# Turning the exponentials of pooled attention in five pieces of 127 and 68 keys instead of six of 96

## The chip, the cores and the metric

One core of a Trainium2 chip runs the whole program. The metric is the device time of one execution in microseconds, as the median of the runs shown; a profile of one further execution gives the rows.

## The reference

Three layers follow each other. Attention comes first, with keys and values pooled by 8, so that each of 8 batches has 8 heads, 576 queries and only 72 keys:

```python
Sp = S // pool                                   # 576 // 8 = 72
k_p = k.reshape(B, H, Sp, pool, D).mean(axis=3)
v_p = v.reshape(B, H, Sp, pool, D).mean(axis=3)
scores = scale * np.matmul(q, k_p.transpose(0, 1, 3, 2))
scores = scores - np.max(scores, axis=-1, keepdims=True)
attn = np.exp(scores)
attn = attn / (np.sum(attn, axis=-1, keepdims=True) + 1e-09)
return np.matmul(attn, v_p).astype(np.float32)
```

Its output, 4608 tokens of 512 numbers, goes through a layer of 8 experts that takes the best one for each token, and then through a second one that takes the best two. Both expert layers multiply by `w1`, take a relu, and multiply by `w2`.

## The kernel before, in words

The attention stage goes over the 4608 tokens in 36 tiles of 128 tokens (a batch is 4.5 tiles, so every ninth tile has its tokens from two batches). The rest of the run is the two expert layers. The order of instructions on every engine is the order in which the code is written; nothing is moved by a scheduler, and waits are put in where a tile's buffer is read or used again.

One step of the attention loop, for token tile t, puts these on TensorE (PE), in this order:

- `transp(t)`: the exponentials of tile t, 128 tokens by 8 heads x 72 keys, are 576 columns. They are turned in six pieces of 96 columns, three into PSUM bank 3 and three into bank 4. ScalarE (ACT) copies each bank to SBUF (`et`, 96 x 384). A piece of 96 keys spans parts of two heads.
- `scores(t+3, 0)`: four heads' scores of a later tile, 4 passes.
- `av(t)`: for each half of the heads (`hb`, 4 heads), three matmuls of the turned exponentials with the prepared `v` block `vb`, into bank 5 or 6. An f32 matmul of this kind is two passes in the trace, a turn is one.
- `scores(t+3, 1)`: the other four heads.
- jobs of the batch to come. In three successive steps ahead of a batch's first tile they are: `place_v` (ACT copies the pooled `v` into a padded layout, two copies), then `prep_v` for half 0, then `prep_v` for half 1. One `prep_v` is four matmuls into bank 7, and one ACT copy that moves the result into `vb`.

ACT does, in one step, the two copies of `transp(t)`, the eight exponentials of tile t+2 (`expo`), and issues the store of tile t-1. VectorE (DVE) takes the maxima, and divides by the sums.

A call of `bank(k)` is a new use of PSUM bank k: its first writer waits until all readers of the bank's last use are through. That is what `bank(3 + hb)` in `transp` and `bank(7)` in `prep_v` do.

Of the kernel before, what the change touches and what calls it, by code (L numbers as in the profile page):

```python
# [41 lines left out]
def kernel(ctx: ExitStack, tc: tile.TileContext, a: dict):  # L42
# [61 lines left out]
    von = rp.tile([96, 6, 2], F32, name="von")  # L104
# [576 lines left out]
    with actx:  # L681
# [7 lines left out]
        for n, t in enumerate((kb[0], vp[0], rc, *kb[1:], *vp[1:])):
            (V if n < 3 else G).memset(t, 0.0)  # L690
        for h in range(2):
            r = slice(64 * h, 64 * h + 64)
            w0 = (1 + h) * VW
            A.activation(rc[r, :, w0:w0 + D], ident[r, 64 * h:64 * h + D].unsqueeze(1).to_broadcast([D, 4, D]), AF.Copy)
            A.activation(rc[r, :, w0 + D:w0 + D + E], wg1[r], AF.Copy)
        for t in vb:
            G.memset(t[96:97], 0.0)
            for c in (0, 2, 3, 5):
                G.memset(t[96:97, c, VW - 1, :], 1e-9)
            G.tensor_copy(t[0:96, :, VW - 1, :], von)  # L700
        for t in (*etb[0], *etb[1]):
            G.memset(t[96:97], 1.0)
# [284 lines left out]
        for t in range(NT):  # L987
# [265 lines left out]
def host_arrays(inp):  # L1253
# [27 lines left out]
    vo = np.zeros((6 * 96, 2), f)  # L1281
    for c in range(6):
        for s in range(96):
            h = (96 * c + s) // 72
            vo[96 * c + s, h - (c % 3) - 4 * (c // 3)] = 1
    r["vones"] = vo.reshape(6, 96, 2).transpose(1, 0, 2)
# [31 lines left out]
```

## Time and profile before

| | |
|---|---|
| median of 3 runs | 1511.95 us (1509.63 to 1512.92) |
| the profiled execution: its own time | 1503.11 us |
| the profiled execution: span from first to last instruction | 1501.4 us |
| PE busy over the span | 1450.4 us, 97% |
| ACT, DVE, POOL busy over the span | 80%, 78%, 60% |
| attention stage: first to last turn of exponentials | 19.5 us to 163.8 us |

The profiled execution is 8.8 us below the median of the runs, of which 1.7 us are outside its span. Busy shares of PE count a matmul until its result is out, and matmuls follow each other before that; so what one costs in a stream is the distance from its start to the next one's start, and not its duration.

### The profile page before, as it was taken

What the parts mean: (1) busy time and instruction counts of PE and PEld (TensorE: products, weight loads), DVE (VectorE), ACT (ScalarE), POOL (GpSimd) and SP (SyncE); (2) the same over time, 40 slices, a digit from 0 to 9 for tenths busy, and PEclk for the clock granted to TensorE, in tenths of its full rate; (3) what the DMA queues carried; (4) which work ended last, traced back from release to release, by engine and by line L of the source; (5) the groups of instructions that cost most, each with busy time, mean ns of one, the idle gap of its engine ahead of it and who ended that gap; (6) DMA issues with size and microseconds to landing.
All of it is one profiled execution on the core that took longest, in us unless ns stands there. A gap on an engine that the chain in (4) does not pass through costs nothing.

```text
span 1501.4 us, 31172 instructions
## 1 busy us (share of the span) xinstructions
PE 1450.4 (97%) x7485; PEld 1206.7 (80%) x7485; DVE 1177.1 (78%) x2990; ACT 1194.4 (80%) x3155; POOL 901.3 (60%) x1065
## 2 busy tenths in 40 slices
PE   5999889999999999999999999999999999999996
PEld 5998768888888888778888888788888888888885
DVE  4778747777777777778888888888888888888883
ACT  5777558888888888778888888888888888888882
POOL 7677757888878888555454444544545444454442
PEclk9999999999999999999999999999999999999999
DMA  8866665655666565544434444344443444434432
GB/s 303 307 236 246 191 186 149 162 159 159 163 155 160 159 163 149 138 107 100 93 87 104 92 105 94 85 106 92 95 102 87 106 92 100 97 87 105 92 99 31
DMA packets 146685, 200.55 MB, mean 134 GB/s; under 512 B 71953, under 2 KB 104977, under 8 KB 143825
## 3 DMA queue, kind: packets, MB, share of 16 engines
q1 hardware_dynamic: 112032, 139.11, 30.6%
q0 software_dynamic: 24688, 49.94, 17.2%
q10 hardware_dynamic: 9792, 9.44, 1.9%
q8 instruction: 80, 1.31, 0.4%
q14 instruction: 93, 0.75, 0.2%
HBM read 121.64 MB, written 62.26 MB: 122 GB/s over the span
## 4 chain that ended last, share of the span: by engine, by line
issue 45%; POOL 29%; POOLq 6%; DMA 5%; PE 5%; DVE 5%; ACT 5%; SPq 0%; ACTq 0%; DVEq 0%
POOL out L453 8%; POOL w2l L223 6%; POOL l_d L187 4%; POOLq L174 3%; ACT xt L289 2%; POOL w1l L223 2%; POOL x L250 2%; POOL nz L254 2%; DMA x_d<-xr 1%; POOLq L223 1%; DMA x3t<-x 1%; POOL cur L244 1%; DVE g2t L393 1%; PE bank L294 1%; POOL x L358 1%
## 5 line engine op out<-in xcount | busy, mean ns | idle before, releaser
L312 DVE STREAM_TRANSPOSE ht<-h 32x256 f32<-32x256 f32 x1136 | 495.3, 436 | 96.6 <-ACT h L305 81.9
L289 ACT ACTIVATE xt<-xz 32x128 f32<-32x128 f32 x1728 | 531.2, 307 | 41.4 <-DVE xz L282 20.2
L294 PE MATMUL bank<-w1h,xh 128*128 (+1 forms) x904 | 357.9, 396 | 3.5 <-ACT xh L274 3.5
L295 PE MATMUL bank<-w1l,xh 128*128 (+1 forms) x904 | 355.2, 393 | 0.0
L296 PE MATMUL bank<-w1h,xl 128*128 (+1 forms) x904 | 354.3, 392 | 0.6 <-DVE xl L278 0.6
L296 PE MATMUL bank<-w2h,hl 128*128 (+1 forms) x896 | 351.7, 393 | 2.2 <-DVE hl L321 1.1
L295 PE MATMUL bank<-w2l,hh 128*128 (+1 forms) x896 | 351.5, 392 | 0.0
L294 PE MATMUL bank<-w2h,hh 128*128 (+1 forms) x896 | 350.7, 391 | 0.0
L223 POOL TENSOR_TENSOR w1l<-sg,w1h 128x512 f32 x109 | 140.7, 1291 | 239.4 <-ACT w1h L220 236.6
L453 POOL DMA_INDIRECT out<-yo,cur x76 | 121.0, 1592 | 161.5 <-ACT yo L450 157.3
L294 PEld LDWEIGHTS bank<-w1h,xh 128*128 128x128 f32 x904 | 170.1, 188 | 40.5 <-ACT xh L274 4.1
L296 PEld LDWEIGHTS bank<-w2h,hl 128*128 128x128 f32 x896 | 168.3, 188 | 42.4 <-DVE hl L321 4.3
L296 PEld LDWEIGHTS bank<-w1h,xl 128*128 128x128 f32 x904 | 170.0, 188 | 38.6 <-DVE xl L278 1.7
L295 PEld LDWEIGHTS bank<-w1l,xh 128*128 128x128 f32 x904 | 170.3, 188 | 35.3
L294 PEld LDWEIGHTS bank<-w2h,hh 128*128 128x128 f32 x896 | 168.3, 188 | 37.4
L295 PEld LDWEIGHTS bank<-w2l,hh 128*128 128x128 f32 x896 | 168.3, 188 | 36.4
L305 ACT ACTIVATE h<-bank 128x512 f32<-128x512 f32 x226 | 132.2, 585 | 55.3 <-PE bank L296 51.5
L223 POOL TENSOR_TENSOR w2l<-sg,w2h 128x512 f32 x109 | 141.5, 1298 | 14.6 <-ACT w2h L220 13.6
L250 POOL DMA_INDIRECT x<-x_d,cur x113 | 124.1, 1098 | 36.1 <-POOL cur L244 33.2
L278 DVE TENSOR_TENSOR xl<-xt,xh 128x512 fp32r<-128x512 f32 x108 | 75.8, 702 | 72.7 <-ACT xh L274 58.6
L320 ACT ACTIVATE hh<-ht 128x1024 fp32r<-128x1024 f32 x71 | 75.5, 1063 | 58.3 <-DVE ht L312 58.3
L187 POOL DMA_INDIRECT l_d<-le,dst x74 | 77.8, 1052 | 52.0 <-DVE dst L443 38.8
(267 smaller groups left out, 1970.2 us busy)
## 6 DMA issues: line engine op xcount, KB each, us to landing
sg<-w SPq DMA_DIRECT2D x118, 512.0 KB, 3.7
x_d<-zt SPq DMA_DIRECT2D x46, 256.0 KB, 2.8
out<-zt SPq DMA_DIRECT2D x37, 256.0 KB, 2.6
x_d<-yo SPq DMA_DIRECT2D x37, 256.0 KB, 2.1
x_d<-xr ACTq DMA_DIRECT2D x36, 256.0 KB, 5.7
kk<-kT SPq DMA_DIRECT2D x7, 1152.0 KB, 5.3
q<-qT SPq DMA_DIRECT2D x7, 1152.0 KB
vv<-vT SPq DMA_DIRECT2D x7, 1152.0 KB, 10.8
```

What stands on the lines that cost most here:

```text
L187: ins = G.indirect_dma_start(out=dram_t, out_offset=bass.IndirectOffsetOnAxis(ap=ix, axis=0), in_=src, in_offset=None, bounds_check=P * LC ...
L223: eng.tensor_tensor(l, u.sg[:, k, :], h.bitcast(F32), op=OP.subtract)
L250: G.indirect_dma_start(out=u.x, out_offset=None, in_=src[0:top, :], in_offset=off, bounds_check=top - 1, oob_is_err=True)
L278: V.tensor_tensor(u.xl, p, u.xh.bitcast(F32), op=OP.subtract)
L289: A.activation(u.xt[32 * q:32 * q + 32, :, 32 * i:32 * i + 32], zv[:, q], AF.Copy)
L294: nc.tensor.matmul(p, hs, rh, start=first, stop=False)
L295: nc.tensor.matmul(p, hs, rl, start=False, stop=False)
L296: nc.tensor.matmul(p, ls, rh, start=False, stop=last)
L305: A.activation(u.h[:, 512 * hf:512 * hf + 512], p, AF.Relu)
L312: V.transpose(out=t[32 * q:32 * q + 32, :, 32 * i:32 * i + 32], in_=hv[:, q])
L320: A.activation(u.hh, u.t, AF.Copy)
L453: G.indirect_dma_start(out=out_d, out_offset=bass.IndirectOffsetOnAxis(ap=u.ci[:, 2:3], axis=0), in_=u.yo, in_offset=None, bounds_check=N ...
```

## The change

The exponentials of a pair of heads are 144 columns. The first 127 of each pair are now one piece each (four pieces), and the last 17 of all four pairs are gathered by DVE into a small tile `el` of 68 columns (`lows`), which makes the fifth piece. `transp` turns that one first, into bank 4, then two pieces into bank 3, then two into bank 4 again. There are three ACT copies in place of two. `lows(t+1)` stands on DVE after the maxima of tile t+3's first half.

`av` keeps three matmuls for each half: one for each pair of heads, and one with the 68 gathered keys, which adds to the second head of both pairs. `prep_v` makes the `v` block to match: two matmuls of 146 columns and two of 73, and two ACT copies instead of one. `place_v` writes three copies in place of two. The constant in row 127 (or 96 before) that adds 1e-9 to the sums is kept in another row.

```diff
+MR = 127
+CUT = MR - SP_
+LK = SP_ - CUT
+LR = 4 * LK
+LB = MR + 3 * LK
+LW = LB + LR
...
-        etb = [[wk.tile([97, 3, P], F32, name=f"et{n}{hb}", bufs=1) for hb in range(2)] for n in range(2)]
-        rc = rp.tile([P, 4, 4 * VW], F32, name="rc")
+        etb = [wk.tile([P, 5, P], F32, name=f"et{n}", bufs=1) for n in range(2)]
+        rc = rp.tile([P, 4, 2 * VW], F32, name="rc")
...
         def place_v(b, prs=slice(0, 4)):
             for h in range(2):
                 r = slice(64 * h, 64 * h + 64)
-                A.activation(vp[b % 2][r, prs, 48 + 72 * h:120 + 72 * h], vk[b][r, prs], AF.Copy, scale=1.0 / POOL)
+                for s0, s1, c0 in ((0, SP_, 0),) if h == 0 else ((0, CUT, SP_), (CUT, SP_, LB)):
+                    A.activation(vp[b % 2][r, prs, c0:c0 + s1 - s0], vk[b][r, prs, s0:s1], AF.Copy, scale=1.0 / POOL)
...
         def prep_v(b, hb):
             v, o = vp[b % 2], vb[b % NB]
-            pv = bank(7)[0:96, 0:6 * VW].rearrange("p (c w) -> p c w", c=3)
-            ev, od = 2 * hb, 2 * hb + 1
-            nc.tensor.matmul(pv[:, 0, :], v[:, ev, 48:144], rc[:, ev, VW:3 * VW], start=True, stop=True)
-            nc.tensor.matmul(pv[:, 1, :], v[:, ev, 144:240], rc[:, ev, 2 * VW:4 * VW], start=True, stop=False)
-            nc.tensor.matmul(pv[:, 1, :], v[:, od, 0:96], rc[:, od, 0:2 * VW], start=False, stop=True)
-            nc.tensor.matmul(pv[:, 2, :], v[:, od, 96:192], rc[:, od, VW:3 * VW], start=True, stop=True)
-            A.activation(o[0:96, 3 * hb:3 * hb + 3, 0:VW - 1, :].rearrange("p c w h -> p c h w"),
-                         pv.rearrange("p c (h w) -> p c h w", w=VW)[:, :, :, 0:VW - 1], AF.Copy)
+            pv = bank(7)[:, 0:6 * VW].rearrange("p (c h w) -> p c h w", c=3, h=2)
+            for j in range(2):
+                pr = 2 * hb + j
+                nc.tensor.matmul(flat(pv[0:MR, j]), v[:, pr, 0:MR], rc[:, pr, :], start=True, stop=True)
+            for j in range(2):
+                pr = 2 * hb + j
+                nc.tensor.matmul(pv[0:LR, 2, j, :], v[:, pr, LB - LK * pr:LB - LK * pr + LR], rc[:, pr, VW:],
+                                 start=True, stop=True)
+            A.activation(o[0:MR, 2 * hb:2 * hb + 2, 0:VW - 1, :].rearrange("p c w h -> p c h w"),
+                         pv[0:MR, 0:2, :, 0:VW - 1], AF.Copy)
+            A.activation(o[0:LR, 4 + hb, 0:VW - 1, :].rearrange("p w h -> p h w"), pv[0:LR, 2, :, 0:VW - 1], AF.Copy)
...
+        def lows(t):
+            if t >= NT:
+                return
+            los[t] = wk.tile([P, LR], F32, name="el")
+            V.tensor_copy(los[t].rearrange("p (c k) -> p c k", c=4),
+                          es[t].rearrange("p a (c h) s -> p (a c) (h s)", h=2)[:, :, MR:])
+
         def transp(t):
-            e = es.pop(t).rearrange("p a h s -> p (a h s)")
+            e = es.pop(t).rearrange("p a (c h) s -> p (a c) (h s)", h=2)
             et = etb[t % 2]
+            p = bank(4)[0:LR, 2 * P:3 * P]
+            nc.tensor.transpose(p, los.pop(t), ident)
+            A.activation(et[0:LR, 4], p, AF.Copy)
             for hb in range(2):
-                p = bank(3 + hb)[0:96, 0:3 * P].rearrange("p (c t) -> p c t", c=3)
-                for c in range(3):
-                    cc = 3 * hb + c
-                    nc.tensor.transpose(p[:, c, :], e[:, 96 * cc:96 * cc + 96], ident)
-                A.activation(et[hb][0:96], p, AF.Copy)
+                p = bank(3 + hb)[0:MR, 0:2 * P].rearrange("p (c t) -> p c t", c=2)
+                for c in range(2):
+                    nc.tensor.transpose(p[:, c, :], e[:, 2 * hb + c, 0:MR], ident)
+                A.activation(et[0:MR, 2 * hb:2 * hb + 2], p, AF.Copy)
             ets[t] = et
...
                     for c in range(3):
-                        r = 96 if c == 1 else 97
-                        nc.tensor.matmul(p[r0:r0 + n, :, c:c + 2],
-                                         et[hb][0:r, c, r0:r0 + n], vb[b % NB][0:r, 3 * hb + c],
+                        r, k, heads = (P, 2 * hb + c, slice(2 * c, 2 * c + 2)) if c < 2 else (LR, 4, slice(1, 4, 2))
+                        nc.tensor.matmul(p[r0:r0 + n, :, heads],
+                                         et[0:r, k, r0:r0 + n], vb[b % NB][0:r, k + (hb if c == 2 else 0)],
                                          start=(c == 0), stop=(c == 2), skip_group_check=True)
```

On PE, before the change, a tile whose step follows a `prep_v` job reads as follows (first the four matmuls of `prep_v`, then the six turns, then the first scores of a later tile; the number after `bank` is the PSUM bank, the second number the use of it):

```order
L743 MATMUL bank7_502<-rc_158,vp1_150 96x146
L744 MATMUL bank7_502<-rc_158,vp1_150 96x146
L745 MATMUL bank7_502<-rc_158,vp1_150 96x146
L746 MATMUL bank7_502<-rc_158,vp1_150 96x146
L799 MATMUL bank3_515<-ident_sb_94,e_417 96x128 x3
L799 MATMUL bank4_520<-ident_sb_94,e_417 96x128 x3
L772 MATMUL bank0_526<-kb1_147,q_105 128x144 x2
```

With the change the same place, one tile earlier, reads as follows; a name in brackets is the semaphore of the engine that the instruction waits for.

```order
L749 MATMUL bank7_446<-rc_156,vp1_150 127x146 x2
L752 MATMUL bank7_446<-rc_156,vp1_150 68x73 x2
L813 MATMUL bank4_459<-ident_sb_94,el_415 68x128 [waits DVE_49,PE_49]
L818 MATMUL bank3_462<-ident_sb_94,e_363 127x128 x2
L818 MATMUL bank4_466<-ident_sb_94,e_363 127x128 [waits Activation_49]
```

The gathered piece takes bank 4 first (use 459); the pieces of the second two pairs take it again (use 466), and their first turn waits for ACT.

On ACT the same two places read, before (the copy of `vb`, the two copies of `et`, the exponentials, the store):

```order
L747 ACTIVATE vb_152<-bank_502 96x3x2x72
L800 ACTIVATE et_154<-bank_515 96x384
L800 ACTIVATE et_155<-bank_520 96x384
L788 ACTIVATE e<-bank_469,mx 128x72 x4
L788 ACTIVATE e<-bank_498,mx 128x72 x4
L829 DMA x_d<-xr 256x1x256
```

and with the change:

```order
L754 ACTIVATE vb_152<-bank_446 127x2x2x72
L756 ACTIVATE vb_152<-bank_446 68x2x72
L814 ACTIVATE et_155<-bank_459 68x128
L819 ACTIVATE et_155<-bank_462 127x256
L819 ACTIVATE et_155<-bank_466 127x256
L796 ACTIVATE e<-bank_411,mx 128x72 x4
L796 ACTIVATE e<-bank_442,mx 128x72 x4
L848 DMA x_d<-xr 256x1x256
```

There are two copies out of bank 7 where there was one, and both stand ahead of the copy of the gathered piece (from use 459 of bank 4).

## Rows read from the trace of the kernel before

**Rows 1.** The page: PE's busy time, and its share in 40 slices with the clock.

```profile
PE 1450.4 (97%) x7485; PEld 1206.7 (80%) x7485; DVE 1177.1 (78%) x2990; ACT 1194.4 (80%) x3155; POOL 901.3 (60%) x1065
...
PEclk9999999999999999999999999999999999999999
```

**Rows 2.** Busy us of each engine in three stretches of the attention stage, clock, DMA share.

```profile
40.00:80.00 40.00, 38.85 (x341) 37.18 (x340) 29.64 (x92) 29.27 (x111) 25.49 (x33) 1.00 0.85 317
80.00:120.00 40.00, 39.13 (x333) 37.29 (x332) 30.52 (x97) 29.22 (x110) 29.85 (x39) 1.00 0.71 249
120.00:160.00 40.00, 37.20 (x319) 35.10 (x318) 33.00 (x115) 29.25 (x110) 29.10 (x40) 1.00 0.63 223
```

**Rows 3.** Timeline of PE, four tiles from 84 us: start, us, what.

```profile
84.03 0.82 PE L799 MATMUL bank<-ident_sb,e 128*96 128x128 f32 x6
84.69 0.66 PE L772 MATMUL bank<-kb,q 128*128 128x144 f32 x4
85.18 1.75 PE L818 MATMUL bank<-vb,et 97*128 97x146 f32 x12
86.76 0.66 PE L772 MATMUL bank<-kb,q 128*128 128x144 f32 x4
87.25 0.82 PE L799 MATMUL bank<-ident_sb,e 128*96 128x128 f32 x6
...
90.57 0.41 PE L743 MATMUL bank<-rc,vp 128*96 128x146 f32 x2
90.82 0.41 PE L744 MATMUL bank<-rc,vp 128*96 128x146 f32 x2
...
91.56 0.82 PE L799 MATMUL bank<-ident_sb,e 128*96 128x128 f32 x6
...
95.83 0.82 PE L799 MATMUL bank<-ident_sb,e 128*96 128x128 f32 x6
...
99.10 0.49 PE L799 MATMUL bank<-ident_sb,e 128*96 128x128 f32 x3
```

**Rows 4.** Timeline of ACT in the same stretch; idle before it in brackets.

```profile
84.62 0.86 ACT L800 ACTIVATE et<-bank 96x384 f32<-96x384 f32 x2 [0.70 <-PE bank L799]
...
85.38 1.77 ACT L788 ACTIVATE e<-bank,mx 128x72 f32<-128x72 f32 x8
87.00 0.91 ACT L737 ACTIVATE vp<-vk 64x288 f32<-64x288 f32 x2
87.93 0.86 ACT L800 ACTIVATE et<-bank 96x384 f32<-96x384 f32 x2
...
91.76 0.56 ACT L747 ACTIVATE vb<-bank 96x432 f32<-96x432 f32 x1 [1.14 <-PE bank L746]
92.21 0.85 ACT L800 ACTIVATE et<-bank 96x384 f32<-96x384 f32 x2
...
99.69 0.86 ACT L800 ACTIVATE et<-bank 96x384 f32<-96x384 f32 x2 [0.70 <-PE bank L799]
```

**Rows 5.** Timeline of PE's weight loads: the first of `av` in the tile from 91.56.

```profile
92.74 1.55 PEld L818 LDWEIGHTS bank<-vb,et 97*128 97x128 f32 x12
```

**Rows 6.** Groups of instructions by shape, 40 to 160 us: busy us, mean ns.

```profile
L788 ACT ACTIVATE e<-bank,mx 128x72 f32<-128x72 f32 x241 | 53.8, 333 | 2.1 <-DVE mx L780 1.9
...
L800 ACT ACTIVATE et<-bank 96x384 f32<-96x384 f32 x60 | 25.8, 481 | 11.5 <-PE bank L799 11.3
L799 PE MATMUL bank<-ident_sb,e 128*96 128x128 f32 x182 | 25.0, 273 | 0.0
...
L747 ACT ACTIVATE vb<-bank 96x432 f32<-96x432 f32 x13 | 7.4, 567 | 17.4 <-PE bank L746 15.1 <-PE bank L799 2.3
...
L823 DVE TENSOR_REDUCE lg<-xr 128x8 f32<-128x64 f32 x30 | 6.6, 220 | 1.0
...
L737 ACT ACTIVATE vp<-vk 64x288 f32<-64x288 f32 x12 | 5.4, 448 | 0.1
```

**Rows 7.** Who waited for whom, 40 to 160 us: us in total, times, longest.

```profile
PEld bank L818 <- ACT et L800: 3.9, 4, 1.2
PEld L865 <- issue: 1.9, 4, 1.1
...
PE bank L818 <- DVE rs L821: 1.8, 2, 1.0
```

More of the change, by code (lines that the diff above doesn't have):

```diff
@@ L103 @@
     wg1 = cload("wg1", [P, 4, E], pool=rp)
-    von = rp.tile([96, 6, 2], F32, name="von")
+    von = rp.tile([P, 6, 2], F32, name="von")
     nc.sync.dma_start(von, a["vones"])
@@ L684 @@
         kb = [rp.tile([P, 4, 144], F32, name=f"kb{n}") for n in range(NB)]
-        vp = [rp.tile([P, 4, 240], F32, name=f"vp{n}") for n in range(2)]
-        vb = [ap1.tile([97, 6, VW, 2], F32, name=f"vb{n}") for n in range(NB)]
-        etb = [[wk.tile([97, 3, P], F32, name=f"et{n}{hb}", bufs=1) for hb in range(2)] for n in range(2)]
-        rc = rp.tile([P, 4, 4 * VW], F32, name="rc")
+        vp = [rp.tile([P, 4, LW], F32, name=f"vp{n}") for n in range(2)]
+        vb = [ap1.tile([P, 6, VW, 2], F32, name=f"vb{n}") for n in range(NB)]
+        etb = [wk.tile([P, 5, P], F32, name=f"et{n}", bufs=1) for n in range(2)]
+        rc = rp.tile([P, 4, 2 * VW], F32, name="rc")
         for n, t in enumerate((kb[0], vp[0], rc, *kb[1:], *vp[1:])):
@@ L692 @@
             r = slice(64 * h, 64 * h + 64)
-            w0 = (1 + h) * VW
+            w0 = h * VW
             A.activation(rc[r, :, w0:w0 + D], ident[r, 64 * h:64 * h + D].unsqueeze(1).to_broadcast([D, 4, D]), AF.Copy)
@@ L696 @@
         for t in vb:
[L697 to L702, printed above, removed]
+            G.memset(t[96:128], 0.0)
+            G.tensor_copy(t[:, :, VW - 1, :], von)
+        for t in etb:
+            G.memset(t[96:128], 1.0)
         def pool_k(b, eng, prs=range(4)):
@@ L790, in expo @@
             es[t] = e
+        los = {}
+        def lows(t):
[4 more added lines that the diff above has]
+                          es[t].rearrange("p a (c h) s -> p (a c) (h s)", h=2)[:, :, MR:])
         def transp(t):
-            e = es.pop(t).rearrange("p a h s -> p (a h s)")
+            e = es.pop(t).rearrange("p a (c h) s -> p (a c) (h s)", h=2)
             et = etb[t % 2]
+            p = bank(4)[0:LR, 2 * P:3 * P]
+            nc.tensor.transpose(p, los.pop(t), ident)
+            A.activation(et[0:LR, 4], p, AF.Copy)
             for hb in range(2):
-                p = bank(3 + hb)[0:96, 0:3 * P].rearrange("p (c t) -> p c t", c=3)
-                for c in range(3):
-                    cc = 3 * hb + c
-                    nc.tensor.transpose(p[:, c, :], e[:, 96 * cc:96 * cc + 96], ident)
-                A.activation(et[hb][0:96], p, AF.Copy)
+                p = bank(3 + hb)[0:MR, 0:2 * P].rearrange("p (c t) -> p c t", c=2)
+                for c in range(2):
+                    nc.tensor.transpose(p[:, c, :], e[:, 2 * hb + c, 0:MR], ident)
+                A.activation(et[0:MR, 2 * hb:2 * hb + 2], p, AF.Copy)
             ets[t] = et
@@ L979 @@
         prep_v(0, 0)
+        lows(0)
         transp(0)
@@ L995 @@
             maxes(t + 3, 0)
+            lows(t + 1)
             expo(t + 2)
@@ L1280, in host_arrays @@
     r["bias"] = np.broadcast_to(inp["moe_modality_bias"][None], (P, 2, E))
[L1281 to L1286, printed above, removed]
+    vo = np.zeros((P, 6, 2), f)
+    vo[0:SP_, 0:4, 0] = vo[SP_:MR, 0:4, 1] = 1
+    vo[MR, 0:4] = 1e-9
+    for pr in range(4):
+        vo[LK * pr:LK * pr + LK, 4 + pr // 2, pr % 2] = 1
+    r["vones"] = vo
     p = np.arange(P)
```

## The prediction

> **What bounds the kernel now.** I read the page first: PE is busy 97% of the span, and its clock is full in all slices [rows 1]. Next the attention stage in stretches of 40 us, since the change touches nothing else: PE is busy 37 to 39 of 40 us, ACT 29, DVE 30 to 33, POOL 25 to 30, and the clock is 1.00 [rows 2], the higher of its two levels. A busy PE can still be waiting, so I then read the timeline for distances from start to start [rows 3]. A tile that neither follows nor precedes `prep_v` takes 3.22 us (84.03 to 87.25): turns 0.66, scores 0.49, `av` 1.58, scores 0.49. A turn is (0.82 - 0.273)/5 = 0.109 us [rows 3, 6]. A `prep_v` matmul is 0.25 (90.57 to 90.82), so 1.00 for four. Twelve `av` passes at the pace of the scores, (0.66 - 0.29)/3 = 0.124, would be 1.49; the 0.09 left over is a wait for the copy of `et`: in the tile from 91.56 the copy starts at 92.21, lasts 0.48, and the weight load of `av` starts 0.05 after its end, at 92.74 [rows 4 to 6]. All else on PE is end to end. What PE issues, and what makes it pause inside a tile, is therefore the time of this stage.
>
> The tiles come in four kinds, by what ACT does at the first turn (time T) and whether a `prep_v` follows:
> - plain: 3.22 us; ACT stands idle until the copies (0.70 idle) [rows 3, 4].
> - after `place_v`, with a `prep_v`: 87.25 to 91.56, 4.31 us. ACT is in `place_v` until T + 0.66 (87.91).
> - after a `prep_v`, with another: 91.56 to 95.83, 4.27 us. ACT copies `vb` from T + 0.20 to T + 0.76.
> - after the second `prep_v`: 95.83 to 99.10, 3.27 us. ACT is again in the copy of `vb` [rows 3, 4].
> Batches 1 to 7 give 7 tiles each of the last three kinds; 15 are plain, and the first three of these I leave out as they wait for the first loads.
>
> **What the change removes.** One turn in six: 0.11 a tile, which leaves 0.55. In `prep_v`, two of four matmuls go from 146 to 73 columns. No f32 row has that size; bounds are 0.25 (as now) and half of it. I take half, the cost of a pass following its columns as in turns and scores: 0.75 instead of 1.00. PE's own work is then 0.55 + 0.49 + 1.49 + 0.49 = 3.02 a tile, plus 0.75 with `prep_v`.
>
> **What it adds: a wait of PE for ACT in the middle of the turns.** The gathered piece is turned first, into bank 4, and the second two pairs take bank 4 again, so their first turn waits for the ACT copy of the gathered piece, in the same tile. The order of PE shows it: the turn into use 466 waits for ACT; before, neither group of three did. Behind it on PE stand the scores, `av` and all that follows. The wait W is worked out on the plain tile. A turn lasts 0.273 [rows 6], and ACT starts 0.10 after the last turn's end (99.10 + 0.49 = 99.59, copy at 99.69) [rows 3, 4], so the copy starts at T + 0.37. It moves 128 columns. Nearest rows: the copy of 384 columns at 0.48, `place_v`'s of 288 at 0.448, exponentials of 72 at 0.333, or 0.20 apart in a row of eight ((1.77 - 0.33)/7) [rows 4, 6]. On the line through 384 and 288 it would be 0.39, on the line through 567 (432 columns) and 481 (384) it would be 0.02; I take 0.28, between 0.20 and 0.48. Then 0.05 until the weight load, as above, and some 0.04 because that load is not hidden behind a running matmul (chosen; a load is 1.55/12 = 0.13 at most [rows 5]). PE goes on at T + 0.74. Without the wait it would do so after three turns, T + 0.33. **W = 0.41.** `av` no longer waits for `et`: its copy ends near T + 1.0, and PE reaches `av` at 0.55 + 0.41 + 0.49 = 1.45, so the 0.09 goes. Plain tile: 3.02 + 0.41 = 3.43, **+0.21**.
>
> Where ACT is busy at T, the gathered copy queues behind it, since ACT works in order.
> - After `prep_v` there are now two copies out of bank 7 ahead of it, 288 and 144 columns. With 0.45 (the row of 288) and 0.30 (between 0.20 and 0.45), overlapping by 0.11 as now (91.76 + 0.56 against 92.21), they run from T + 0.20 to T + 0.84; the gathered copy from 0.73 to 1.01; PE goes on at 1.10. W = 0.77. Tile with a `prep_v`: 3.02 + 0.75 + 0.77 = 4.54, **+0.27**; without: 3.79, **+0.52**.
> - After `place_v`, three copies (288, 220, 68 columns) where two took 0.91: some 0.2 more, of which a longer tile gives back a little. End T + 0.80, gathered copy until 1.05, PE on at 1.14. W = 0.81. Tile: 3.02 + 0.75 + 0.81 = 4.58, **+0.27**.
>
> **Sum:** 12 x 0.21 + 7 x (0.27 + 0.27 + 0.52) = 2.5 + 7.4 = +9.9 us. With W of the kinds open this is 12 W1 + 7 (W2 + W3 + W4) - 11.4, which is zero at a mean W of 0.35. Part is absorbed where PE already waits for chains that it doesn't set: 3.9 + 1.9 + 1.8 = 7.6 us in the stage [rows 7]; I take 2, bounds 0 and 7.6. Left: **+8 us**.
>
> By the ScalarE: Activation LUTs page of the Trainium skill (What ACT_TABLE_LOAD costs), an ACTIVATE with immediate scale costs 186 ns and 0.833 ns for each column; an estimate from it is 293 ns for the gathered copy, and the sum would be 33 x 0.013 = 0.4 us higher. It gives 506 ns for 384 columns, where the trace has 481.
>
> **What I cost at nothing.** DVE's gather is 0.2 a tile (nearest row: the sum of 64 columns into `lg`, 0.22 [rows 6]); DVE has 7 to 10 us of 40 idle [rows 2], and its result is wanted a step later. With that cover gone it is 36 x 0.2 = 7 us. ACT's copies of `et`: 640 columns in three instead of 768 in two, about even. No DMA is added but 32 rows of a small constant; `av` has the same passes of 146 columns. The expert layers start when the last tile's experts are known, and PE has no less to do there, so a later end of attention passes on in full.
>
> **The rivals.**
> - *Small wait*: the copies that now stand ahead cost the wait nothing (ACT finishes them in the time that the longer tile gives). W = 0.41 everywhere: 33 x 0.41 - 11.4 = +2, less 2 absorbed: 1512. For it: in plain tiles ACT has 0.70 idle [rows 4]. Against: ACT starts the `vb` copy at T + 0.20 because it waits for PE's last `prep_v` matmul, and that comes right ahead of T, however long the tile.
> - *Faster*: the result of the gathered turn is signalled and copied so soon that PE hardly stops. It decides at a mean W below 0.35, and shows as faster below 0.25. At 0.15: 5 - 11.4 = -6.4, 1505.5. For it: 68 weight columns instead of 96, and exponentials 0.20 apart. Against: 0.37 from turn to ACT is the same in all rows of a free ACT, and a lone copy lasts its full time, not its pace; the least that the rows give is W = 0.37 + 0.20 + 0.09 - 0.33 = 0.33 in plain tiles, more in the others.
> - *Larger wait*: copies at their longest rows, without overlap (0.57 twice and 0.48; 0.45 more after `place_v`): W = 0.63, 1.60, 1.60, 1.36, so 39.5 - 11.4 = +28; with nothing saved in `prep_v` (14 x 0.25) +31.5: 1543.
> - *Hidden*: loads set the pace (DMA share 0.85 in the first stretch [rows 2]), and the stage stays as long: 1512. Against it: PE's timeline has no gap for loads in the four tiles read.
>
> A rule bears on whether the wait must be there at all, since the two uses of bank 4 have different columns. The PSUM — Partial Sum Buffer page of the Trainium skill (PSUM bank collisions raise a hardware error) says that two engines on one bank and one group of 32 partitions at once is an error, and that semaphores should guard banks, not addresses. By it the wait belongs to this choice of banks; without the wait the sum would be -11.4 plus 33 x 0.09 for `av`'s old wait, -8.4. The order of PE has the wait; no run here shows a collision.
>
> **How the numbers follow.** Forecast, +3 to +14 around +8: 0.68. Small wait 0.11, hidden 0.06, faster 0.06, larger (over +14) 0.09. The sum is against the profiled execution, 1503.1 us, which would be 1511; that execution is 8.8 below the median of 1511.95, and on the median I predict **1520 us**. Range 1513 to 1529: it leaves out the faster rival, part of the hidden and small ones, and the far end of the larger one. The bounds with all copies at their shortest (W = 0.33, 0.63, 0.57, 0.57: +5, 7.6 absorbed) are 1509, at their longest 1543. What a measurement can tell from no change is 0.2%, 3 us: faster 0.06, same 0.16 (the small and hidden cases mostly), slower 0.78.
>
> **What would show it.** Right: distances of 3.4 between first turns of plain tiles, 4.5 and 3.8 for the others; a weight load of the second two pairs' turns that starts 0.05 after the gathered copy ends, in nearly every tile; no wait of `av` for `et`; `prep_v` at 0.75. Wrong: plain tiles at 3.1 or less, a gathered copy well under 0.28, or PE waiting elsewhere, for DVE's gather above all. The forecast fails if tiles grow as said but the expert layers don't start later.

## The result, and the profile after

The change makes the kernel slower: 1528.98 us, the median of 5 runs (1525.96 to 1537.80), against 1511.95 (1509.63 to 1515.25); the ratio is 1.0123, interval 1.0109 to 1.0137. By the medians that is +17.0, by the ratio +18.6, where +8 was forecast and 1513 to 1529 was the range. The profiled execution of the change is its longest, 1537.80 with a span of 1536.1; a second profile of the same kernel (below, *again*) took 1517.79. I read the single tile in the first and add the stages up in the second.

The page of the kernel after, PE's busy time and its clock in 40 slices, against [rows 1]:

```profile
PE 1462.9 (95%) x7449; PEld 1210.6 (79%) x7449; DVE 1189.9 (77%) x3026; ACT 1200.5 (78%) x3216; POOL 903.6 (59%) x1051
...
PEclk8999999999999999999999999999999999999998
```

The same stretches as [rows 2]. PE was at 37.2 to 39.1 of 40 us; it is at 33 to 36, the clock is no longer 1.00 throughout, and no other engine has filled up: PE waits.

```profile
40.00:80.00 40.00, 36.25 (x304) 33.12 (x303) 30.30 (x97) 29.44 (x121) 25.28 (x33) 1.00 0.74 278
80.00:120.00 40.00, 33.04 (x261) 30.28 (x260) 29.34 (x88) 26.14 (x109) 28.05 (x37) 0.94 0.72 255
120.00:160.00 40.00, 33.59 (x273) 30.73 (x272) 28.43 (x97) 25.08 (x103) 27.64 (x35) 0.98 0.61 199
```

PE's timeline after, against [rows 3]: a plain tile (49.23 to 52.73), one after `place_v` (from 56.55), one after a `prep_v` (from 60.84) and one after the second `prep_v` (65.40 to 69.22).

```profile
49.23 0.27 PE L813 MATMUL bank<-ident_sb,el 128*68 128x128 f32 x1
49.34 0.39 PE L818 MATMUL bank<-ident_sb,e 128*127 128x128 f32 x2
49.92 0.49 PE L818 MATMUL bank<-ident_sb,e 128*127 128x128 f32 x2 [0.20 <-ACT et L814]
50.25 0.66 PE L780 MATMUL bank<-kb,q 128*128 128x144 f32 x4
...
52.73 0.27 PE L813 MATMUL bank<-ident_sb,el 128*68 128x128 f32 x1
...
57.28 0.49 PE L818 MATMUL bank<-ident_sb,e 128*127 128x128 f32 x2 [0.23 <-ACT et L814]
...
60.84 0.27 PE L813 MATMUL bank<-ident_sb,el 128*68 128x128 f32 x1
...
61.84 0.49 PE L818 MATMUL bank<-ident_sb,e 128*127 128x128 f32 x2 [0.51 <-ACT et L814]
...
65.40 0.27 PE L813 MATMUL bank<-ident_sb,el 128*68 128x128 f32 x1
...
66.41 0.49 PE L818 MATMUL bank<-ident_sb,e 128*127 128x128 f32 x2 [0.52 <-ACT et L814]
...
69.22 0.27 PE L813 MATMUL bank<-ident_sb,el 128*68 128x128 f32 x1
```

The reader is to see the hole after the third turn in each: PE goes on 0.69, 1.00 and 1.01 us after the tile's first turn, where three turns in a stream would be through at 0.33. The distances are 3.50, 4.56 and 3.82, against 3.22, 4.27 and 3.27 in [rows 3]. ACT's timeline says what is waited for, against [rows 4]: the gathered copy starts 0.37 after the first turn where ACT is free (49.60), and 0.68 after it where the two copies of `vb` stand ahead (61.52).

```profile
49.60 0.27 ACT L814 ACTIVATE et<-bank 68x128 f32<-68x128 f32 x1 [1.16 <-PE bank L813]
...
61.04 0.44 ACT L754 ACTIVATE vb<-bank 127x288 f32<-127x288 f32 x1 [0.97 <-PE bank L752]
61.36 0.27 ACT L756 ACTIVATE vb<-bank 68x144 f32<-68x144 f32 x1
61.52 0.26 ACT L814 ACTIVATE et<-bank 68x128 f32<-68x128 f32 x1
```

Groups by shape, 40 to 160 us, against [rows 6]: the gathered copy's mean is 0.272, the gather's (L806) 0.337, and the weight loads of `av` (L837) wait 0.4 us for `et`. Then the waits, against [rows 7], where `av` waited 3.9 us for `et`: now the weight load of the second two pairs' first turn waits, 25 times, for the gathered copy.

```profile
L837 PEld LDWEIGHTS bank<-vb,et 128*128 128x128 f32 x184 | 26.9, 196 | 0.6 <-ACT et L819 0.4 <-issue 0.2
...
L806 DVE COPY el<-e 128x68 f32<-128x68 f32 x26 | 8.8, 337 | 0.0
...
L814 ACT ACTIVATE et<-bank 68x128 f32<-68x128 f32 x26 | 7.1, 272 | 10.5 <-PE bank L818 5.1 <-PE bank L813 4.8 <-PE bank L780 0.5
```

```profile
PEld bank L818 <- ACT et L814: 15.9, 25, 1.6
```

All this is as the prediction has it, but for the gather's mean, which it put at 0.2. What it doesn't have stands in other rows. At the start of attention DVE's gather of tile 0 takes 2.64 us, and in tile 19 two operations of the gate, 0.20 to 0.25 each where nothing holds them, take 2.61 and 1.44. In both places POOL sums up `k` at the same time. DVE, then POOL, of the kernel after:

```profile
18.47 2.64 DVE L806 COPY el<-e 128x68 f32<-128x68 f32 x1
...
110.16 2.61 DVE L865 TENSOR_TENSOR geq<-lg,gm 128x72 f32<-128x72 f32 x1
112.81 1.44 DVE L866 TENSOR_TENSOR geq<-geq,cst_sb 128x72 f32<-128x72 f32 x1
114.28 0.23 DVE L868 TENSOR_REDUCE gmi<-geq 128x9 f32<-128x72 f32 x1
```

```profile
18.44 2.62 POOL L712 TENSOR_TENSOR pool<-kk 128x1152 f32<-128x1152 f32 x1
...
110.06 2.62 POOL L712 TENSOR_TENSOR pool<-kk 128x1152 f32<-128x1152 f32 x1 [5.38 <-DMA kk<-kT]
112.76 1.40 POOL L713 TENSOR_TENSOR pool<-pool 128x576 f32<-128x576 f32 x1
```

DVE's operation ends within 0.1 us of POOL's each time (21.11 and 21.06; 112.77 and 112.68; 114.25 and 114.16). A sum over one input (L868) beside POOL's next sum keeps its 0.23, and operations that read PSUM keep theirs (0.46 for the product `xr`, beside such a sum and without one). PE waits for the gate 2.93 us and has the clock's lower level, 1.2 GHz, for the next 7 (0.51); tiles 19 and 20 take 7.81 and 6.86 where the kernel before has 4.03 and 4.23. In the kernel before the two don't meet: the gate comes 9.0 us earlier, POOL's sum, which waits for a load, only 4.3. PE and the window of the kernel after, then DVE and POOL of the kernel before:

```profile
115.17 0.47 PE L884 MATMUL bank<-goh,tri_bf 128*128 128x72 bf16 x9 [2.93 <-DVE goh L870]
```

```profile
114.80:121.80 7.00, 6.48 (x34) 6.08 (x34) 5.45 (x26) 3.00 (x12) 4.41 (x8) 0.51 0.75 275
```

```profile
101.20 0.23 DVE L846 TENSOR_TENSOR geq<-lg,gm 128x72 f32<-128x72 f32 x1
```

```profile
105.80 2.64 POOL L708 TENSOR_TENSOR pool<-kk 128x1152 f32<-128x1152 f32 x1 [5.38 <-DMA kk<-kT]
```

The Trainium skill's page VectorE: DVE Perf Modes (Two Vector instructions with no wait between them) has an operation with two SBUF inputs, and one that runs in a two-port mode, read through a second SBUF interface that is shared with GpSimd. The rows shown agree for the operations with two inputs; whether the copy runs in such a mode, no row says. That page of the Trainium skill gives no price, and the rows give one of up to 2.6 us.

### The profile page after: what moved, and what is told of

Its sections match the earlier page's. It is cut to its first block, busy times and chain, and to the rows that moved or that the text cites. A ratio compares the mean times of both kernels' runs of the same rounds, so it can differ in the third digit from the quotient of the medians.

```text
span 1536.1 us, 31196 instructions
## 1 busy us (share of the span) xinstructions
PE 1462.9 (95%) x7449; PEld 1210.6 (79%) x7449; DVE 1189.9 (77%) x3026; ACT 1200.5 (78%) x3216; POOL 903.6 (59%) x1051
## 4 chain that ended last, share of the span: by engine, by line
issue 39%; POOL 20%; PE 19%; ACT 8%; DVE 5%; POOLq 5%; DMA 2%; SPq 1%; another core or an unknown queue 0%; ACTq 0%; DVEq 0%
POOL out L459 8%; POOL w2l L229 6%; ACT xt L295 4%; PE bank L300 3%; PE bank L302 3%; PE bank L301 3%; POOLq L180 3%; PE bank L837 3%; PE bank L780 2%; PE bank L818 1%; POOL l_d L193 1%; DVE g2t L399 1%; POOL w1l L229 1%; POOL x L256 1%; POOLq L229 1%
## 5 line engine op out<-in xcount | busy, mean ns | idle before, releaser
L229 POOL TENSOR_TENSOR w2l<-sg,w2h 128x512 f32 x109 | 141.5, 1298 | 12.5 <-ACT w2h L226 12.1
L193 POOL DMA_INDIRECT l_d<-le,dst x74 | 80.9, 1093 | 51.1 <-DVE dst L449 37.9
```

Source lines behind the costliest of these rows:

```text
L193: ins = G.indirect_dma_start(out=dram_t, out_offset=bass.IndirectOffsetOnAxis(ap=ix, axis=0), in_=src, in_offset=None, bounds_check=P * LC ...
L229: eng.tensor_tensor(l, u.sg[:, k, :], h.bitcast(F32), op=OP.subtract)
```

## The experiments

Each timing stands beside the kernel before on the same chip. "Start" is the first turn of tile 2; "usual" is tiles 2 to 31 (9 plain, 7 of each other kind) at the shortest length that a tile of the kind has in that execution, or the second shortest where the shortest stands alone; "beyond" is what these tiles took over it; "end" is tiles 32 to 34. The four add up to the first turn of tile 35. A row is one profiled execution, and the split between "usual" and "beyond" is good to about 2 us, since tiles of a kind differ by up to 0.3. The profiles of e2, e7 and e11 are the fastest of their runs, and from tile 35 to its end a profile takes between 1332.9 and 1345.0 us, so a row and its median can differ by some us.

| kernel | median, before beside it | ratio (interval) | start | usual | beyond | end | tile 35 |
|---|---|---|---|---|---|---|---|
| before | 1511.95 | | 32.7 | 113.3 | 7.7 | 9.5 | 163.2 |
| after | 1528.98, 1511.95 | 1.0123 (1.0109 to 1.0137) | 35.9 | 121.8 | 21.3 | 12.7 | 191.8 |
| again (the change) | 1517.51, 1503.30 | 1.0087 (1.0070 to 1.0104) | 35.0 | 121.6 | 8.5 | 12.7 | 177.8 |
| e1_bank3 | 1506.87, 1503.30 | 1.0018 (1.0004 to 1.0032) | 36.4 | 107.3 | 13.6 | 11.7 | 169.0 |
| e2_wait_alone | 1512.44, 1503.30 | 1.0062 (1.0046 to 1.0078) | 31.4 | 122.8 | 4.9 | 10.0 | 169.2 |
| e3_scores_between | 1513.80, 1503.30 | 1.0076 (1.0055 to 1.0098) | 34.4 | 112.0 | 13.7 | 12.5 | 172.6 |
| e4_bank3_act_gather | 1516.84, 1510.69 | 1.0040 (1.0023 to 1.0056) | 33.2 | 110.0 | 24.7 | 11.1 | 179.0 |
| e5_change_act_gather | 1532.05, 1510.69 | 1.0138 (1.0109 to 1.0167) | 32.0 | 124.7 | 21.1 | 10.6 | 188.4 |
| e6_gather_alone | 1511.99, 1510.69 | 1.0006 (0.9990 to 1.0021) | 32.6 | 113.4 | 11.9 | 10.4 | 168.3 |
| e7_bank3_ends | 1507.45, 1504.65 | 1.0020 (1.0010 to 1.0030) | 31.9 | 107.3 | 12.9 | 10.3 | 162.4 |
| e8_change_ends | 1518.14, 1504.65 | 1.0085 (1.0068 to 1.0102) | 34.6 | 121.6 | 8.6 | 12.6 | 177.5 |
| e9_act_splits | 1505.63, 1504.65 | 1.0000 (0.9991 to 1.0008) | 32.4 | 113.7 | 7.6 | 9.5 | 163.2 |
| e10_before_again | 1504.87, 1504.65 | 1.0005 (0.9995 to 1.0015) | 31.0 | 113.3 | 7.8 | 9.5 | 161.7 |
| e11_change_pool_pieces | 1513.50, 1504.26 | 1.0078 (1.0050 to 1.0106) | 32.9 | 121.6 | 5.7 | 12.7 | 172.9 |
| e12_before_pool_pieces | 1505.28, 1504.26 | 1.0011 (1.0001 to 1.0021) | 30.9 | 113.4 | 8.4 | 9.5 | 162.2 |
| e13_bank3_ends_xr6 | 1502.33, 1504.26 | 0.9994 (0.9984 to 1.0003) | 33.2 | 107.4 | 12.6 | 10.9 | 164.0 |
| e14_bank3_ends_xr6_pieces | 1504.32, 1504.26 | 1.0004 (0.9990 to 1.0018) | 33.1 | 107.3 | 11.7 | 10.3 | 162.5 |

### Is it the wait in the turns?

*again* is the change, unchanged, as the measure for the others.

> The changed kernel once more, nothing else. Theory A (all of the loss comes from PE's wait for ACT in the middle of the turns; about +10 us of it is the wait itself, seen in the tile distances, and the rest, some 7, is what such gaps bring along: the lower clock and jobs that move against each other): ratio near 1.012 again, tile distances 3.50, 4.60, 4.56 and 3.81 again, but the long tiles (7.8, 6.9, 12.1, 6.4 us) differ in place or size from the first profile. Theory B (the part over +10 has a cause of its own in the DVE gather or the added ACT copies): the long tiles stand in the same places with the same causes.

The long tiles stand where they stood (0, 19, 20, 26 and 34), but for tile 29, which takes 4.26 us instead of 12.08. That is theory B for the most part.

*e1_bank3* turns the gathered piece into bank 3, with the first two pairs; bank 4 has one use in a tile, and nothing waits inside the turns.

```diff
-            p = bank(4)[0:LR, 2 * P:3 * P]
-            nc.tensor.transpose(p, los.pop(t), ident)
-            A.activation(et[0:LR, 4], p, AF.Copy)
             for hb in range(2):
+                k = bank(3 + hb)
+                if hb == 0:
+                    nc.tensor.transpose(k[0:LR, 2 * P:3 * P], los.pop(t), ident)
...
+                if hb == 0:
+                    A.activation(et[0:LR, 4], k[0:LR, 2 * P:3 * P], AF.Copy)
```

> The gathered piece is turned into bank 3, in one use with the first two pairs, and its copy follows theirs; bank 4 has the second two pairs alone. PE has nothing to wait for in the turns; gather, copies and v block stay as in the change. Theory A: the whole loss goes and the saved turn and the shorter matmuls show: 6 to 10 us under the kernel before, ratio 0.993 to 0.996; plain tiles at 3.1. Theory B: the 7 us stay, so that it ends near the kernel before, -1 +- 2 us.

PE's timeline of e1_bank3: five turns in a stream, 0.55 us, and a plain tile of 3.12.

```profile
47.94 0.27 PE L815 MATMUL bank<-ident_sb,el 128*68 128x128 f32 x1
48.05 0.61 PE L818 MATMUL bank<-ident_sb,e 128*127 128x128 f32 x4
48.49 0.66 PE L780 MATMUL bank<-kb,q 128*128 128x144 f32 x4
...
51.06 0.27 PE L815 MATMUL bank<-ident_sb,el 128*68 128x128 f32 x1
```

*e2_wait_alone* is the kernel before, with the last of its six pieces turned first into a use of bank 4 of its own, with a copy of its own. *e3_scores_between* is the change with `scores(t+3, 0)` put between the turns of the first two pairs and those of the second two, so that PE has work while ACT copies.

```diff
+            p = bank(4)[0:96, 2 * P:3 * P]
+            nc.tensor.transpose(p, e[:, 480:576], ident)
+            A.activation(et[1][0:96, 2], p, AF.Copy)
             for hb in range(2):
-                p = bank(3 + hb)[0:96, 0:3 * P].rearrange("p (c t) -> p c t", c=3)
-                for c in range(3):
+                n = 3 - hb
+                p = bank(3 + hb)[0:96, 0:n * P].rearrange("p (c t) -> p c t", c=n)
+                for c in range(n):
```

> The kernel before with the wait alone: of its six pieces of 96 the last is turned first, into a use of bank 4 of its own with its own copy; then three into bank 3, then two into bank 4. No gather, v block as before. The first piece's copy has three turns of PE's time to hide in, not two. Worked out by the tile with what the change's profile shows (copy at T + 0.37 for 0.27, weights not hidden 0.10): plain +0.27, the other three kinds +0.5. Theory A: 12 x 0.27 + 21 x 0.5 = +13.6 us directly, and some 5 of followers, ratio 1.009 to 1.014. Theory B: +13 us at most, with no clock loss beyond that of the kernel before.

```diff
             for hb in range(2):
+                if hb and t:
+                    scores(t + 3, 0)
                 p = bank(3 + hb)[0:MR, 0:2 * P].rearrange("p (c t) -> p c t", c=2)
```

> The change with the first half of the scores moved between the turns of the first two pairs and those of the second two (same banks, same wait): 0.49 us of PE work covers the wait. Theory A: the wait is 0 in plain tiles and about 0.2 in the others, and nearly all of the loss goes: 4 to 8 us under the kernel before, ratio 0.995 to 0.997. Theory B: +1 us or more over the kernel before.

Taking the wait out of the change gives 10.6 us back (1517.51 to 1506.87); putting it alone into the kernel before costs 9.1, less than theory A had, and makes the usual tiles 9.5 longer (122.8). So the wait is the change's main cost, two thirds to three quarters of the 14.2 that *again* lost. But e1_bank3's tiles are 6.0 shorter than before's, and its median is still 3.6 above; "start", "beyond" and "end" took it all back. e3_scores_between hides most of the wait too (112.0), and loses more than half of that in "beyond" (13.7 against 8.5 in *again*); its median is 3.7 better than that of *again*, where 4 to 8 under the kernel before were expected. The theory that the wait is all falls.

### Is the rest the gather?

*e4* is e1_bank3 and *e5* the change with the gather on ACT, right behind the same tile's exponentials; *e6* is the kernel before with its last piece of 96 copied to `el` by DVE and turned from there.

```diff
-            V.tensor_copy(los[t].rearrange("p (c k) -> p c k", c=4),
+            A.activation(los[t].rearrange("p (c k) -> p c k", c=4),
```

> As the kernel with the gathered piece in bank 3 (no wait in the turns), and the gather of the 17 left keys is done by ACT, right behind the exponentials of the same tile, instead of DVE. Theory C (beside PE's wait, some 10 us of the loss come from the gather's place on DVE: it is held up to 2.6 us while POOL runs a long tensor_tensor, and stands behind other DVE work in the first and the last tile, and PE waits for it): 4 to 9 us under the kernel before, ratio 0.994 to 0.997; first turn at 19.4 us again, plain tiles still 3.1, step from tile 34 to 35 near 3.4. Theory D (the shortfall comes from the other parts, that is the added ACT copies, the new v block or the new layout in memory): +2 us over the kernel before, as with the gather on DVE.

> The change as it is, with PE's wait, and only the gather moved from DVE to ACT. Theory C: 8 to 10 us less than the change, so +3 to +6 us over the kernel before, ratio 1.002 to 1.004. Theory D: no better than the change, +13 us.

```diff
+            los[t] = wk.tile([P, 96], F32, name="el")
+            V.tensor_copy(los[t], es[t].rearrange("p a h s -> p (a h s)")[:, 480:576])
...
-                    nc.tensor.transpose(p[:, c, :], e[:, 96 * cc:96 * cc + 96], ident)
+                    nc.tensor.transpose(p[:, c, :], el if cc == 5 else e[:, 96 * cc:96 * cc + 96], ident)
```

> The kernel before with the gather alone: the last of its six pieces of 96 columns is copied by DVE into a small tile first, at the same place on DVE as in the change, and turned from there; turns, banks, copies and v block as before, no wait in the turns. Theory C: +5 to +10 us over the kernel before, ratio 1.003 to 1.007, the first turn near 21 us, DVE copies of up to 2.6 us beside POOL's tensor_tensor. Theory D: 0 to +2 us.

The gather on ACT doesn't help, and a gather alone costs nothing that can be told (+0.9 by the ratio, interval from -1.5 to +3.2), though five of its 36 gathers take 1.1 to 2.4 us. But e6 turns the gathered piece last and not first, and its gather of tile 0 is not held (0.20); so it doesn't try what happens at the first tile of the change. *e7* and *e8* move only the gathers of tiles 0 and 35 to ACT, in e1_bank3 and in the change.

```diff
+            src = es[t].rearrange("p a (c h) s -> p (a c) (h s)", h=2)[:, :, MR:]
+            if t in (0, NT - 1):
+                A.activation(dst, src, AF.Copy)
+            else:
+                V.tensor_copy(dst, src)
```

> The kernel of e1_bank3 (no wait of PE inside the turns), with the gathers of tile 0 and tile 35 alone done by ACT right after those tiles' exponentials; the other 34 stay on DVE. Theory G (at the two ends of attention PE waits for DVE's gather, which is held beside POOL's sums in tile 0 and stands behind subtractions in tile 35; in e1 the first two tiles were 3.7 us late and the last four 2.2 us longer than before): about -3 us against the kernel before, 5 to 6 us under e1, and no stretch of lower clock at 20 us. Theory R (the rest sits in the copies of ACT and in the new block of v, or in stalls that move from run to run): +2 to +4, as e1.

> The change as it is (with PE's wait inside the turns), with the gathers of tile 0 and tile 35 alone done by ACT. Theory G: 4 to 5 us less than the change (which was +13 and +17 against the kernel before), so about +8 to +12, the forecast of the tiles alone; first turn of tile 0 near 19.5 us instead of 21.2, and the distance from tile 34 to 35 near 3.8 us instead of 6.3. Theory R: +13 to +17, as the change.

In the one profile of e7_bank3_ends the start and the end are shorter as expected (31.9 and 10.3), but its median isn't (+2.8; e1_bank3 had +3.6); e8_change_ends keeps both. At the start its first turn does come earlier, at 19.73 instead of 21.27, but from 20.4 on the clock is at its lower level for 10.2 us (0.50), and tile 2 starts at 34.6 all the same. So the longer start isn't shown to be the gather's. The last two tiles of *again* show why the end stays. Three engines, DVE, ACT and PE:

```profile
175.16 2.36 DVE L238 TENSOR_TENSOR w1l<-sg,w1h 128x1024 fp32r<-128x1024 f32 x2 [0.81 <-ACT w1h L237]
177.44 0.19 DVE L806 COPY el<-e 128x68 f32<-128x68 f32 x1
```

```profile
171.92 1.11 ACT L237 ACTIVATE w1h<-sg 128x1024 fp32r<-128x1024 f32 x1
172.87 0.30 ACT L814 ACTIVATE et<-bank 68x128 f32<-68x128 f32 x1
```

```profile
173.22 0.49 PE L818 MATMUL bank<-ident_sb,e 128*127 128x128 f32 x2 [1.28 <-ACT et L814]
...
177.78 0.40 PE L813 MATMUL bank<-ident_sb,el 128*68 128x128 f32 x1 [2.52 <-DVE rs L840]
```

The weights of the next layer are being split there, on ACT (L237) and on DVE (L238). The gathered copy stands behind the first, and the gather behind the second. With the gather on ACT the second wait goes and the first grows to 2.11 us (PE's row at 174.11 in e8_change_ends): the wait in the turns meets whatever ACT has in hand.

*e9* has ACT's added copies alone, in the kernel before; *e10* is the kernel before again.

```diff
+                for s0, s1 in ((0, SP_),) if h == 0 else ((0, 55), (55, SP_)):
...
+            for c0, c1 in ((0, 2), (2, 3)):
+                A.activation(o[0:96, 3 * hb + c0:3 * hb + c1, 0:VW - 1, :].rearrange("p c w h -> p c h w"),
```

> The kernel before with two of ACT's copies cut up as in the change: the second half of v is placed in two pieces of 55 and 17 keys, and each eviction of v's block is two copies (two pieces, then one). No gather, six turns, no new wait of PE inside the turns. Theory R (part of the loss is ACT's added copies): +3 to +8 us. Theories A and G: 0 to +1, since ACT has idle time in each tile and the two extra copies delay the copies of et only in 21 tiles, by 0.2 to 0.3 us that av would wait: at most 21 x 0.25 = 5 us if none of it is hidden.

> The kernel before, unchanged, profiled once more on this chip: 0, within 0.2%. What it tells: how much the sum of the tiles 2 to 31, the first two tiles, the last four and the long single tiles (over 5 us) vary from one profiled execution to the next with nothing changed. If they vary by under 1 us, the differences of 2 to 6 us that the runs with the gather show there belong to the gather; if by several, they don't.

The copies cost nothing without a wait behind them, and the kernel before repeats itself but for its first two tiles (1.7; there the first profile has 3.4 us of the lower clock, 0.51, and e10 none). So the 3 us more at the change's end, and the 5 to 6 beyond in e1_bank3 and e7, belong to the change.

### POOL's sums, and the stores

*e11* and *e12* cut POOL's first two sums of `k` into pieces of 288 columns, in the change and in the kernel before. *e13* is e7_bank3_ends with six buffers for `xr` instead of four, *e14* that with the pieces.

```diff
-            eng.tensor_tensor(t1, src[:, 0:4, c], src[:, 4:8, c], op=OP.add)
-            eng.tensor_tensor(t1[:, 0:2, :], t1[:, 0:2, :], t1[:, 2:4, :], op=OP.add)
+                for i in range(4):
+                    eng.tensor_tensor(t1[:, i, :], src[:, i, c], src[:, 4 + i, c], op=OP.add)
+                for i in range(2):
+                    eng.tensor_tensor(t1[:, i, :], t1[:, i, :], t1[:, 2 + i, :], op=OP.add)
```

> The change, with POOL's sums of k cut up: the first sum of 1152 columns in four of 288, the second of 576 in two; nothing else. Theory H (DVE's operations that read SBUF twice or copy SBUF to SBUF stand still until POOL's sum beside them ends: 2.6 us for 1152 columns; so the gather of tile 0 is 2.4 us long, and the gate at tiles 19 and 20 late by 3): no DVE operation is held longer than about 0.8 us, tiles 19 and 20 together 3 us shorter, the start 1.5 us earlier: 3 to 5 us less than the change, so +8 to +11 against the kernel before where the change was +13. Rival (the holds are only beside each other, or PE waits for something else there): +13 to +17 as before; POOL's added instructions, some 0.2 us each, cost nothing or a little.

> The kernel before, with POOL's sums of k cut up in the same way. Control: if theory H holds, PE's short waits for the gate at tiles 10, 26 and 28 (1.0, 0.8 and about 1 us) shrink, -1 to -2 us; otherwise 0. If this gains as much as e11 does over the change, the cut helps any kernel and doesn't explain what the change lost.

```diff
-            xr = wk.tile([P, 2, D + E, 4], F32, name="xr", bufs=4)
+            xr = wk.tile([P, 2, D + E, 4], F32, name="xr", bufs=6)
```

> The kernel of e7_bank3_ends with six buffers instead of four for the attention results that a store empties. There PE ran ahead and tile 10 took 6.8 us against 5.0, of which DVE stood 2.95 us for a store to free its buffer. Theory S (stores set that wait): tile 10 near 4.0 to 5.0, 2 us less than e7: 0 to +1 against the kernel before. Rival (the load beside it sets the pace, the wait moves to it): +2.8 as e7.

> e13 with POOL's sums cut up as in e11. If H and S both hold: tiles 10, 26, 27 and 28 lose 2 + 1.5 + 1.7 + 0.5 us of what e7 had over its usual length, so 4 to 6 us under e7, -1 to -3 against the kernel before: the steady tiles' -6 would then arrive for the most part. If neither: +2 to +3.

In e11_change_pool_pieces the gather of tile 0 takes 0.59 where it took 2.4 to 2.6. In tile 19 the pieces were not put to the test: gate and gather were through at 107.57, 0.40 before POOL's sums of `k` began. DVE, then POOL:

```profile
18.78 0.59 DVE L812 COPY el<-e 128x68 f32<-128x68 f32 x1
...
107.39 0.18 DVE L812 COPY el<-e 128x68 f32<-128x68 f32 x1
```

```profile
107.97 3.05 POOL L714 TENSOR_TENSOR pool<-kk 128x288 f32<-128x288 f32 x4 [5.88 <-DMA kk<-kT]
```

The start is 2.1 earlier than in *again*, tiles 19 and 20 take 8.90 us together instead of 11.96, and the first turn of tile 35 comes 4.9 earlier. The median is +9.2 where the change was +14.2 and e8_change_ends +13.5; by the ratios it is +11.7 against +13.1 and +12.8. e11's six runs spread from 1507.59, the profiled one, to 1525.46, and its interval overlaps theirs. In the kernel before the pieces gain nothing (e12, +1.0), where the theory had 1 to 2 less. So H is shown in the trace for tile 0; at tiles 19 and 20 the gain is that DVE and POOL didn't meet, and what the pieces are worth in the median is not shown. Nor do pieces always free DVE. In e11 itself the gather of tile 26 takes 2.42, where none over 0.8 was expected, and in e14 DVE's operation went on through three of POOL's four:

```profile
125.31 2.73 DVE L879 TENSOR_TENSOR geq<-lg,gm 128x56 f32<-128x56 f32 x1
```

```profile
125.57 3.12 POOL L714 TENSOR_TENSOR pool<-kk 128x288 f32<-128x288 f32 x4
```

Theory S holds for the wait. In tile 10 of e7_bank3_ends DVE's product waits 2.95 us until a store has emptied its buffer; in e13 it starts 0.21 after the row ahead of it begins. DVE of e7, then of e13:

```profile
59.93 0.18 DVE L848 RECIPROCAL rs<-bank 128x4 f32<-128x4 f32 x1 [0.37 <-PE bank L845]
63.06 0.46 DVE L849 TENSOR_TENSOR xr<-bank,rs 128x288 f32<-128x288 f32 x1 [2.95 <-DMA x_d<-xr]
```

```profile
61.25 0.18 DVE L848 RECIPROCAL rs<-bank 128x4 f32<-128x4 f32 x1 [0.18 <-PE bank L845]
61.46 0.46 DVE L849 TENSOR_TENSOR xr<-bank,rs 128x288 f32<-128x288 f32 x1
```

Tile 10 goes from 6.84 to 5.44 (4.0 to 5.0 was expected), and the ratio from 1.0020 to 0.9994, with intervals that don't meet. The profiles don't show where that came from: e13's reaches tile 35 later than e7's (164.0 against 162.4). That is the best version found, and it is no faster than the kernel before beyond what can be told. Tiles 26 to 28 still hold 5.6 us beyond their length in e13 (gate behind POOL's sums, and its followers), and the pieces of e14 didn't free them: its expectation fails.

## Why the prediction was right in direction and wrong in size

- **PE bounds the stage, and what makes it pause inside a tile is its time.** Right. From tile 35 to the end, *again* takes 1338.2 us and the kernel before 1338.1: in these profiles the later end of attention passes on in full.
- **The wait W.** Right in mechanism, kinds and nearly in size. PE goes on at T + 0.69 plain (0.74 foreseen), 1.00 and 1.01 behind `prep_v` (1.10). Behind `place_v` 1.14 was foreseen; with the overlap of 0.11 that the working has behind `prep_v` it would have been 1.06. It is 1.04 in tiles 16 and 25 of the first profile, which take 4.60, and 0.70 to 0.82 in four others, the tile shown (4.29) among them. What came out below was given back by the weight load: the next turn follows at 0.21 instead of 0.11, so 0.10 is not hidden where I took 0.04. Tiles grew by 0.28, 0.03 to 0.29, 0.29 and 0.55 where I had 0.21, 0.27, 0.27 and 0.52. The tiles at a batch's border, which I did not hold apart, grew by 0.67. With these lengths tiles 2 to 31 grow by 9 x 0.28 + 4 x 0.03 + 10 x 0.29 + 3 x 0.55 + 4 x 0.67 = 9.9, and by the sum's terms they would by 9 x 0.21 + 7 x 1.06 = 9.3: the wait was not what was mis-sized. The table's column, which goes by the shortest tiles, has 8.3 (121.6 - 113.3).
- **The copies and the small passes.** 0.272 for the gathered copy against 0.28; `prep_v` at 0.75 (60.09 to 60.84), as assumed. The estimate from ScalarE: Activation LUTs (What ACT_TABLE_LOAD costs) in the Trainium skill, 293 ns, is 8% above the row.
- **Two us absorbed.** The waits of tiles 10, 22, 28 and 29 shrank from 5.5 to 1.6 us, so some 4 were absorbed. But as much and more came in new: 3.4 in tiles 19 and 20, 1.4 elsewhere. "Beyond" is 8.5 against 7.7.
- **What was costed at nothing: the step that failed.** The prediction gave the gather 0.2 a tile on an engine with time to spare, and no wait of PE. DVE's gather is 0.15 to 0.19 most of the time, but 0.4 to 2.6 in 8 of 36 tiles of *again*, and what a held DVE makes PE wait for was in no term, nor was it in the bound of 36 x 0.2. In *again* PE waits 1.50 us for the gather of tile 0, and 1.75 for what stands on DVE behind the gather of tile 20, held for 2.60; in the first profile it was the gate of tile 19 that was held. PE, then DVE and POOL of *again*:

```profile
21.27 0.43 PE L813 MATMUL bank<-ident_sb,el 128*68 128x128 f32 x1 [1.50 <-DVE el L806]
...
112.19 0.27 PE L813 MATMUL bank<-ident_sb,el 128*68 128x128 f32 x1 [1.75 <-DVE rs L840]
```

```profile
109.38 2.62 POOL L712 TENSOR_TENSOR pool<-kk 128x1152 f32<-128x1152 f32 x1 [5.69 <-DMA kk<-kT]
109.45 2.60 DVE L806 COPY el<-e 128x68 f32<-128x68 f32 x1
```

  At the end the gathered copy and the gather stand behind the splitting of weights, and PE waits 1.28 and 2.52. By the table's columns *again* has +2.3 at the start, +0.8 beyond and +3.2 at the end, and 8.3 + 2.3 + 0.8 + 3.2 = 14.6 against +14.2 by its median: on that chip the forecast missed 6 of 14. The traces show these waits; what each is worth in the median, no run settles, since e7, e8 and e11, which take some of them away, can't be told from the kernels that they were made from.
- **The chip of the result.** There the change was +17.0 by the medians. Its profile has a stall in tile 29 that *again* has not: ACT stands 5.21 us, DVE 2.31 and 2.18, and PE behind them, and the tile takes 12.08 us instead of 4.26. ACT of the kernel after:

```profile
163.11 0.27 ACT L814 ACTIVATE et<-bank 68x128 f32<-68x128 f32 x1 [5.21 <-remote]
```

  The profiles of e4 and e5 have a tile 29 of 11.45 and 12.07, with ACT standing 5.16 and 4.61 us. They have no gather on DVE, and e4 no wait in the turns, so neither is the cause. All three stand beside a kernel before at 1510.69 or 1511.95; of the profiles beside one near 1504, none has a tile 29 over 5.5 (e6, beside the one at 1510.69, has 7.19). What stops the engines there stays open; so does why the change costs 3 us more on one chip than on the other, and that its median fell just inside the range there is luck.
- **The rivals.** None came. Small wait and faster fail by the measured W, and hidden by the stage's later end. The time on the first chip, over +14, is the larger rival's, but its mechanism isn't: the wait was not larger, other waits came beside it. "PE waiting elsewhere, for DVE's gather above all" was among the signs of a wrong forecast, and it is what happened, without a price. The rule of the PSUM — Partial Sum Buffer page of the Trainium skill (PSUM bank collisions raise a hardware error), that banks need the guard and not addresses, fits: with another bank the wait is gone and tiles 2 to 31 are 6.0 shorter. No run here shows a collision. The -8.4 foreseen without the wait did not come: the median of e1_bank3 is +3.6.

## What to carry to other kernels

An operation that is put on an idle engine costs nothing only if nothing else of that engine or its neighbours can hold it: look up what stands ahead of it in the queue at the start and the end of the stage, and which long sums POOL runs beside it. A wait for an engine in the middle of a stream on the bounding engine costs the longest work that this engine may have in hand, not the usual one. And an engine made faster soon meets the next limit: e1_bank3 saved 6 us in its tiles and lost more than that at the start, at a store's buffer, at the gate and at the end.

## What was unexpected of the hardware

A DVE copy of 68 columns from SBUF to SBUF took 2.64 us beside a POOL sum of 2.62, while DVE's work out of PSUM went on beside such sums at its length. Cutting that sum into four brought the same copy to 0.59. The clock's lower level (0.51) came after a single stop of PE, 2.93 us long in tile 19, and tile 20 took 6.86 us at it instead of 4.23.
